# Nyström attention and a gated MLP in one program: two batches per inverse iteration, an inverse root moved to GpSimd

## The chip, the cores and the metric

The program runs on one core of a Trainium2 chip. The metric is the device time of one launch in microseconds (us). The core has five engines with a queue each: TensorE (PE in the profile; PEld is its weight load), VectorE (DVE), ScalarE (ACT), GpSimd (POOL) and SyncE (SP), which issues the DMAs here. The engines wait for one another by semaphores. SBUF is the memory on the core, PSUM the banks that TensorE writes.

## What is computed

Eight batches with eight heads go through an approximate attention, whose output is the input of a gated MLP on 4608 tokens (cut from the reference):

```
q, k, v: [8, 8, 576, 64]; m = 32 landmarks, each the mean of 18 rows
A  = softmax(q @ k_lm.T)       # 576 x 32
Bm = softmax(q_lm @ k_lm.T)    # 32 x 32
C  = softmax(q_lm @ k.T)       # 32 x 576
Z  = Bm.T / (norm1(Bm) * norminf(Bm) + 1e-6)
for _ in range(6):
    Z = 2 * Z - Z @ Bm @ Z
attn = A @ Z @ C @ v           # per batch and head; heads side by side: x, 4608 x 512
xn   = x / sqrt(mean(x * x) + 1e-6) * rms_g
out  = (silu(xn @ w_gate) * (xn @ w_val)) @ w_out    # 512 -> 1536 -> 512
```

The weights come as float64 and are decoded on the chip. Products that need it are made in three passes of a high and a low part (hi and lo).

## The kernel before, in words

The MLP runs in two parts. In the first part ("early"), nine chunks of 512 tokens go through a third of the hidden width (four slices of 128). In the second part, from about 485 us on, all tokens go twice through the other two thirds (the names px, pz, pw, swfs). The change touches nothing of the second part.

A chunk (`mlp_chunk`, L252) is a stream of matmuls: psg and psv of each slice, then pso. It needs the normalised x of its tokens as xhi and xlo. Batches have 576 tokens and chunks 512, so chunk i needs batch i (and the end of batch i-1). The attention of later batches is laid into the chunks' matmul streams.

**The order of work** is written by a planner at build time, the class `Mixer` (L212). It keeps a clock and a list of streams (Python generators). `fill` takes a chunk's matmuls one after the other, adds 0.216 to the clock for each, and gives every stream a turn. A stream issues some instructions and then yields: a pair (cost, wait) adds the cost to the clock and puts the stream off by wait times `slack`; a negative number only puts it off. `drain` jumps the clock ahead until a condition holds. `slack` is 1.8 up to chunk 0 and 1.3 from there. TensorE's instructions keep this order. The other engines' instructions are ordered by the framework's scheduler; the streams `seconds` and `newtons` have high priority (`urgent`). A tile's buffer count (`bufs`) says how many tiles of a name can be alive: the next one waits until the oldest is free.

The streams of the attention, per batch b:

- `stage1(b, g)` for the two halves g of four heads: sums over the landmarks' rows (lmT, L342), scores sC, sA and psB on TensorE, maxima (mx), exponentials on ScalarE (E, eb), Bm (L392), and a transposed copy tA (L395). At its start it issues the loads of the next half's q, k and v.
- `back()` inside it, a stream of its own for each half: softmax of A on tA (maximum L406, subtraction on GpSimd L407, exponential, sum L410, multiplication on GpSimd L414, transposition into AT L416), its split into hi and lo (AS, L418, L419), transposition of E (sE, sF, copied to ET, EL), and pCV = C v, scaled into the right-hand side of PV (L443).
- `newton(b)`: norms of Bm, then five steps that multiply Z's factors and C v together (pn on TensorE, PV on VectorE, L496 to L498), a sixth (VZ, L502), and the product pW with its split Whi, Wlo (L520, L521). Each step waits for the one before.
- `second(b)`: pO = A times that product, for g = 0 and 1, copied to xr (L554) and squared (sq, L556). Then, after a wait of `OWL` (`OWL0` for batch 0), the sums of squares (pss, L562), a transposition (sqT), pms and ms (L571), and the inverse root of ms on 128x18 elements (the loop's body is the four VectorE instructions L578 to L581):

```python
nc.vector.tensor_single_scalar(ri, ms.bitcast(I32), 1, op=ALU.logical_shift_right)
nc.vector.tensor_scalar(ri, ri, -1, 0x5F3759DF, op0=ALU.mult, op1=ALU.add)
for c in (1.0, 0.375**2):
    ...
```

  It is spread over the heads' rows (Rb, L583), transposed (Rt), and multiplied into xr with the gain (L587). xr is stored to DRAM for the second part (L591).
- `finish(b, which)` splits xr into xhi (ScalarE, L614) and xlo (VectorE and GpSimd, L616) of the chunks that it belongs to: chunk b at once, chunk b+1 when chunk b is about to start.

The gates: `firsts` (L638) starts batch b's first half when newton(b-2) is done and its second half when second(b-2) is done (batch 1 at once, batch 2 after newton(1)). `newtons` takes the batches one by one, each after both halves' scores, and waits for both halves' pCV before the steps. `seconds` starts second(b) when newton(b) is done and chunk b-1 has started. After the matmuls of chunk i the loop at L683 drains until second(i+1) is issued.

Of the kernel before, what the change touches and what calls it, by code (L numbers as in the profile page):

```python
# [9 lines left out]
F32 = mybir.dt.float32  # L10
# [8 lines left out]
P = 128  # L19
# [4 lines left out]
OWL0 = 7.0  # L24
# [11 lines left out]
OWL = 7.0  # L36
# [13 lines left out]
TAB = 2  # L50
# [25 lines left out]
TINY = 1.0513759e-09  # L76


@with_exitstack
def nystrom_moe_kernel(  # L80
# [47 lines left out]
    VZ = cst.tile([P, G, 3 * D], F32, name="VZ")  # L128
# [169 lines left out]
    with tc.tile_pool(name="ap", bufs=1, side="right") as ap, tc.tile_pool(  # L298
# [36 lines left out]
        def stage1(b, g):  # L335
            nt = state[b]
            qk = loaded.pop((b, g))
            vt, vl_ = loaded.pop((b, g, "v"))
# [7 lines left out]
            if b > 0 and nxt[0] < B:  # L346
                load_qk(*nxt)
                load_v(*nxt)
# [25 lines left out]
            rs = sm.tile([P, 2], F32, name="rs", tag="rs")  # L374
# [5 lines left out]
            E = ap.tile([P, S], F32, name="E", tag="E", bufs=2)  # L380
# [4 lines left out]
            eb = sm.tile([P, M], F32, name="eb", tag="eb")  # L385
# [6 lines left out]
            (nc.scalar.mul if BMA else nc.vector.tensor_scalar_mul)(nt["Bm"][:, g, :], eb, rs[:, 1:2])  # L392
            tA = ap.tile([P, NB, M], F32, name="tA", tag="tA", bufs=TAB)
            for e in range(2):
                nc.vector.transpose(  # L395
                    tA[:, e * (NB // 2) : (e + 1) * (NB // 2), :].rearrange("p n m -> p (n m)"),
                    sA[e],
                )
            yield 1.3, 0.0
            if g == 1:  # L400
                stage["front"] = b

            def back():
                yield -BW * mix.slack
                mA = sm.tile([P, NB], F32, name="mA", tag="mA")
                nc.vector.tensor_reduce(mA, tA, axis=AX.X, op=ALU.max)  # L406
                nc.gpsimd.tensor_sub(tA, tA, mA.unsqueeze(2).broadcast_to([P, NB, M]))  # L407
                nc.scalar.activation(tA, tA, AF.Exp, scale=SC)
                sumA = sm.tile([P, NB], F32, name="sumA", tag="sumA")
                nc.vector.tensor_reduce(sumA, tA, axis=AX.X, op=ALU.add)  # L410
                nc.vector.tensor_scalar_add(sumA, sumA, 1e-9)
                rA = sm.tile([P, NB], F32, name="rA", tag="rA")
                nc.vector.reciprocal(rA, sumA)
                nc.gpsimd.tensor_mul(tA, tA, rA.unsqueeze(2).broadcast_to([P, NB, M]))  # L414
                AT = ap.tile([P, S], F32, name="AT", tag="AT", bufs=ATB)
                nc.vector.transpose(AT, tA.rearrange("p n m -> p (n m)"))  # L416
                AS = ap.tile([P, 2, S], F32R, name="AS", tag="AS", bufs=ASB)
                nc.scalar.copy(AS[:, 0], AT)  # L418
                nc.vector.tensor_sub(AS[:, 1], AT, AS[:, 0].bitcast(F32))  # L419
                nt["AT"][g] = AS  # L420

                sE = pa.tile([P, 4, P], F32, name="sE", tag="pa")
                for ch in range(4):
                    tp(sE[:, ch], E[:, ch * P : (ch + 1) * P], ident)
                sF = pa.tile([2 * M, P], F32, name="sF", tag="pa")
                tp(sF, E[:, 4 * P :], ident)
                ET = ap.tile([P, 4, P], F32, name="ET", tag="ET", bufs=ETB)
                EL = ap.tile([2 * M, P], F32, name="EL", tag="EL", bufs=ETB)
                nc.scalar.copy(ET, sE)
                nc.scalar.copy(EL, sF)  # L430
                yield 0.65, SW2
                pCV = pa.tile([P, D], F32, name="pCV", tag="pa")
                for ch in range(5):
                    for h in range(4):
                        r = slice(h * M, (h + 1) * M)
                        mm(
                            pCV[r, :],
                            ET[:, ch, r] if ch < 4 else EL[:, r],
# [4 lines left out]
                (nc.scalar.mul if CVA else nc.vector.tensor_scalar_mul)(nt["PV"][:, g, M:], pCV, rs[:, 0:1])  # L443
                yield 0.85, 0.2
                done[b] = done.get(b, 0) + 1
                if done[b] == 2:
                    stage["first"] = b
# [11 lines left out]
        def newton(b):  # L459
            nt = state[b]  # L460
            Bm = nt["Bm"]
            BT = sm.tile([P, 2, M], F32, name="BT", tag="BT", bufs=1)
# [3 lines left out]
            sums = sm.tile([P, 4], F32, name="nsum", tag="nsum")  # L466
            nc.vector.tensor_reduce(
                sums[:, 0:2], Bm, axis=AX.X, op=ALU.add, apply_absolute_value=True
            )
            nc.vector.tensor_reduce(  # L470
                sums[:, 2:4], BT, axis=AX.X, op=ALU.add, apply_absolute_value=True
            )
            sb = sm.tile([P, 4, M], F32, name="nsb", tag="nsb", bufs=1)
            nc.vector.tensor_copy(sb, sums.unsqueeze(2).broadcast_to([P, 4, M]))
            sbt = sm.tile([P, 4, M], F32, name="nsbt", tag="nsbt", bufs=1)
# [578 lines left out]
```

## Time and profile before

| | us |
|---|---|
| median of 3 runs | 1066.85 |
| lowest and highest | 1066.61, 1067.96 |
| profiled execution | 1064.71 |
| its span in the trace | 1062.8 |
| TensorE busy | 992.8 |
| VectorE busy | 743.4 |
| ScalarE busy | 486.7 |
| GpSimd busy | 89.5 |

The profile is of one execution. Its span runs from the first to the last instruction; the execution's own time is 1.9 us longer. The views that are quoted below: a string of 40 digits (busy tenths in 40 slices of 26.6 us); busy time of each engine in chosen stages, with the number of instructions behind it, the clock that TensorE was granted (1.00 is full), the share of the DMA engines and GB/s; waits (engine, line and tile that waited, what released it, total us, times, longest); groups of instructions (line, engine, operation, out<-in, shape, xcount, then busy us and mean ns of one, then idle time before them); and the timeline (start, duration, engine, line, operation, tiles, in brackets the idle time just before it and what ended it).

### The profile page before, as it was taken

The page shows a single profiled execution, that of the slowest core. Times are in us where ns is not written, and L with a number is a line of the kernel's source. Part 1 is how long each engine was busy: PE and PEld are TensorE (multiplying, and loading weights), DVE is VectorE, ACT ScalarE, POOL GpSimd, SP SyncE. Part 2 cuts the span into 40 slices and gives each one's busy share as a digit, 9 for nine tenths or more (in the row PEclk, how much of TensorE's full clock was granted, in tenths as well). Part 3 has the DMA queues.
Part 4 walks back from the last instruction along what each step waited for, and adds up shares of the span by engine and source line. Part 5 has one row for each costly group of instructions (what it writes and reads, how often), then busy time and mean ns, then how long its engine had stood idle before and what let it go on. Part 6 is the DMA issues. An engine that isn't in the chain of part 4 may idle for free.

```text
span 1062.8 us, 17582 instructions
## 1 busy us (share of the span) xinstructions
PE 992.8 (93%) x6918; PEld 833.9 (78%) x6918; DVE 743.4 (70%) x1503; ACT 486.7 (46%) x990; POOL 89.5 (8%) x86
## 2 busy tenths in 40 slices
PE   5639689989989999999999999999999999999998
PEld 3326466556767777787989899998999989899997
DVE  7799586797494551988995675747897475675743
ACT  3534556555454543455645352433744334352431
POOL 2243121211020210100000000000000000000000
PEclk7659889999999999999999999999999999999999
DMA  9244343434140211543533505134250432505122
GB/s 335 100 150 136 133 164 105 153 104 163 43 142 11 86 45 40 187 145 119 189 123 135 178 1 179 51 129 155 64 178 21 159 96 83 179 1 178 50 70 80
DMA packets 62946, 123.82 MB, mean 117 GB/s; under 512 B 5520, under 2 KB 27024, under 8 KB 61840
## 3 DMA queue, kind: packets, MB, share of 16 engines
q1 hardware_dynamic: 62864, 122.71, 34.0%
q8 instruction: 54, 0.88, 0.3%
q14 instruction: 28, 0.23, 0.1%
HBM read 84.94 MB, written 37.75 MB: 115 GB/s over the span
## 4 chain that ended last, share of the span: by engine, by line
PE 72%; DVE 15%; DMA 6%; issue 2%; ACT 2%; POOL 2%; SPq 0%; ACTq 0%; POOLq 0%; DVEq 0%
PE pso L141 23%; PE px L141 18%; PE pz L141 9%; PE psg L141 6%; PE psv L141 5%; PE pw L141 5%; DMA qk<-in_q_dram 2%; PE pO L141 2%; DMA srawv<-in_moe_w_val_dram 1%; DVE lmT L342 1%; PE pn L141 1%; DVE xr L587 1%; DVE h L275 1%; PE sC L141 1%; PE pss L141 1%
## 5 line engine op out<-in xcount | busy, mean ns | idle before, releaser
L141 PE MATMUL pso<-whio,h 128*128 128x512 f32 x288 | 96.2, 402 | 5.8 <-DVE h L275 4.7
L141 PE MATMUL pso<-solo,h 128*128 128x512 f32 x432 | 100.4, 390 | 0.0
L829 ACT CAST x<-xf 128x768 fp32r<-128x768 f32 x84 | 68.1, 833 | 69.7 <-DVE xf L847 54.2
L141 PEld LDWEIGHTS pso<-solo,h 128*128 128x128 f32 x432 | 81.0, 188 | 16.3
L141 PE MATMUL pso<-sowhio,h 128*128 128x512 f32 x288 | 90.9, 390 | 0.0
L141 PE MATMUL psg<-xhi,whig 128*128 128x512 f32 x144 | 60.7, 421 | 25.6 <-ACT xhi L614 25.6
L945 DVE TENSOR_TENSOR ob<-ob,pso 128x512 f32<-128x512 f32 x72 | 48.8, 684 | 49.1 <-PE pso L141 48.1
L830 DVE TENSOR_TENSOR x<-xf,x 128x768 fp32r<-128x768 f32 x84 | 79.2, 953 | 5.0 <-ACT x L829 5.0
L877 DVE TENSOR_TENSOR h<-c,h 128x384 fp32r<-128x384 f32 x96 | 53.2, 555 | 37.3 <-ACT h L876 37.2
L898 ACT COPY c<-px 128x384 f32<-128x384 f32 x48 | 23.1, 481 | 108.6 <-PE px L141 108.6
L141 PEld LDWEIGHTS pso<-whio,h 128*128 128x128 f32 x288 | 53.4, 188 | 20.4 <-DVE h L275 6.0
L876 ACT CAST h<-c 128x384 fp32r<-128x384 f32 x96 | 49.4, 515 | 34.5 <-DVE c L887 28.3
L141 PE MATMUL psg<-xlo,whig 128*128 128x512 f32 x144 | 60.6, 421 | 4.7 <-DVE xlo L616 4.0
L141 PEld LDWEIGHTS pso<-sowhio,h 128*128 128x128 f32 x288 | 54.1, 188 | 11.0
L141 PE MATMUL psg<-xhi,wlog 128*128 128x512 f32 x144 | 60.5, 420 | 0.0
L141 PE MATMUL psv<-xhi,wlov 128*128 128x512 f32 x144 | 58.1, 403 | 0.0
L141 PE MATMUL px<-x,swfs0c 128*128 128x384 f32 x288 | 58.0, 335 | 0.0
L141 PE MATMUL psv<-xlo,whiv 128*128 128x512 f32 x144 | 58.0, 403 | 0.0
L141 PE MATMUL px<-x,swfs1c 128*128 128x384 f32 x288 | 57.8, 334 | 0.1
L141 PE MATMUL px<-x,swfs2c 128*128 128x384 f32 x288 | 57.8, 335 | 0.0
L141 PE MATMUL psv<-xhi,whiv 128*128 128x512 f32 x144 | 57.8, 401 | 0.0
L141 PE MATMUL pso<-wloo,h 128*128 128x512 f32 x144 | 57.4, 398 | 0.0
(224 smaller groups left out, 2231.6 us busy)
## 6 DMA issues: line engine op xcount, KB each, us to landing
xd<-xr SPq DMA_DIRECT2D x8, 1152.0 KB, 4.3
pd<-ob SPq DMA_DIRECT2D x36, 256.0 KB, 2.1
xf<-xd SPq DMA_DIRECT2D x8, 1152.0 KB, 7.5
ob<-pd SPq DMA_DIRECT2D x36, 256.0 KB, 3.5
pe<-ob SPq DMA_DIRECT2D x36, 256.0 KB, 2.6
ob<-pe SPq DMA_DIRECT2D x36, 256.0 KB, 2.8
out_dram<-ob SPq DMA_DIRECT2D x36, 256.0 KB, 2.7
vt<-in_v_dram SPq DMA_DIRECT2D x16, 512.0 KB, 4.0
```

Of the source, the lines that this page charges most:

```text
L141: tc.keep_in_program_order(nc.tensor.matmul(*args, **kw))
L275: nc.vector.tensor_sub(h2, s, h1.bitcast(F32))
L342: nc.vector.tensor_reduce(lmT[:, z], qk[z].rearrange("p h (m c) -> p h m c", c=LM), axis=AX.X, op=ALU.add)
L587: last = nc.vector.scalar_tensor_tensor(xr[:, kk], xr[:, kk], gsb[:, kk : kk + 1], Rt, op0=ALU.mult, op1=ALU.mult)
L829: nc.scalar.copy(t[:, 0], src)
L830: nc.vector.tensor_sub(t[:, 1], src, t[:, 0].bitcast(F32))
L876: nc.scalar.copy(hi, s)
L877: nc.vector.tensor_sub(lo, s, hi.bitcast(F32))
L898: nc.scalar.copy(c1, px)
L945: nc.vector.tensor_add(ob, ob, bank.pop(t))
```

## The change

1. `GROUPS`: batches 3 and 4, and 5 and 6, go through `newton` together. Bm, PV, VZ and all its tiles have room for two batches; `bmm` makes all their matmuls into one bank, and each VectorE instruction covers both. Batches 0, 1, 2 and 7 stay alone.
2. New gates in `firsts`: with the pairs, batch 3 and later wait for second(max(1, b-3)) instead of newton(b-2) and second(b-2); batch 4 also for newton(2).
3. `back` takes both halves of a batch at once from batch 3 (`BOTH`) on, with its waits `BW2` and `SW3`. E, tA, AT and the reciprocals rs become tiles of a whole batch; E and tA have one buffer, where each half had one of two.
4. The split of AT into AS moves out of `back` into a stream `splits` of its own, one batch at a time, after pO of the batch before; AS has one buffer of a whole batch.
5. The loads of v for batch 4 and later move from `stage1` to the end of `back` of the batch before.
6. xr has one buffer instead of two (`XRB`). The W step of `newton` waits until pO of the batch before the group is issued.
7. `OWL` and `OWL0` go from 7 to 3.
8. The inverse root: instead of two rounds of four VectorE instructions, three Newton rounds of four GpSimd instructions. Rb is then a copy on VectorE.

```diff
-OWL0 = 7.0
+OWL0 = 3.0
-OWL = 7.0
+OWL = 3.0
-TAB = 2
+TAB = 1
+XRB = 1
+GROUPS = ((0,), (1,), (2,), (3, 4), (5, 6), (7,))
+BOTH = 3
+SW3 = 2.6
+BW2 = 5.5
...
-    VZ = cst.tile([P, G, 3 * D], F32, name="VZ")
+    VZ = cst.tile([P, 2 * G, 3 * D], F32, name="VZ")
...
                 load_qk(*nxt)
-                load_v(*nxt)
+                if nxt[0] <= BOTH:
+                    load_v(*nxt)
...
+            if g == 0:
+                nt["E"] = ap.tile([P, 2, S], F32, name="E", tag="E", bufs=1)
+                nt["tA"] = ap.tile([P, 2, NB, M], F32, name="tA", tag="tA", bufs=TAB)
+                nt["rs"] = sm.tile([P, 2, 2], F32, name="rs", tag="rs")
+                nt["AT"] = ap.tile([P, 2, S], F32, name="AT", tag="AT", bufs=3)
...
-            mix.add(back())
+            if b < BOTH:
+                mix.add(back(b, nt, g, 1))
+            elif g == 1:
+                mix.add(back(b, nt, 0, 2))
+
+        def back(b, nt, g0, n):
...
+            if n == 2 and b + 1 < B:
+                for g in range(2):
+                    load_v(b + 1, g)
+            yield 0.85 * n, 0.2
...
+        def splits():
+            for b in range(B):
+                while stage["first"] < b or stage["small"] < b - 1:
+                    yield -0.3
+                nt = state[b]
+                AS = nt["AS"] = ap.tile([P, 2, 2, S], F32R, name="AS", tag="AS", bufs=1)
+                for g in range(2):
+                    nc.scalar.copy(AS[:, 0, g], nt["AT"][:, g])
+                    nc.vector.tensor_sub(AS[:, 1, g], nt["AT"][:, g], AS[:, 0, g].bitcast(F32))
+                stage["split"] = b
...
         def bmm(lt, rhs, n, nm):
-            ps = pa.tile([P, 2, n], F32, name=nm, tag="pa")
-            for g in range(2):
+            w = lt.shape[1]
+            ps = pa.tile([P, w, n], F32, name=nm, tag="pa")
+            for g in range(w):
...
-            while stage["first"] < b:
+            while stage["first"] < group[-1]:
                 yield -0.3
...
+            while stage["small"] < group[0] - 1:
+                yield -0.3
...
-            xr = ap.tile([P, NK, S], F32, name="xr", tag="xr", bufs=2)
+            xr = ap.tile([P, NK, S], F32, name="xr", tag="xr", bufs=XRB)
...
+                if g == 1:
+                    stage["small"] = b
                 yield 0.9, ((OWL if b else OWL0) if g == 1 else OW)
...
-            for c in (1.0, 0.375**2):
-                nc.vector.tensor_mul(r2, r1, r1)
-                nc.vector.scalar_tensor_tensor(r2, r2, c, ms, op0=ALU.mult, op1=ALU.mult)
-                nc.vector.scalar_tensor_tensor(r2, r2, -10.0 / 3.0, r2, op0=ALU.add, op1=ALU.mult)
-                nc.vector.scalar_tensor_tensor(r1, r2, 5.0, r1, op0=ALU.add, op1=ALU.mult)
+            for _ in range(3):
+                nc.gpsimd.tensor_mul(r2, r1, r1)
+                nc.gpsimd.tensor_mul(r2, r2, ms)
+                nc.gpsimd.tensor_scalar(r2, r2, -0.5, 1.5, op0=ALU.mult, op1=ALU.add)
+                nc.gpsimd.tensor_mul(r1, r1, r2)
...
-            (nc.scalar.mul if RBA else nc.vector.tensor_scalar_mul)(Rb, r1.unsqueeze(2).broadcast_to([P, NB, M]), 0.375**2)
+            nc.vector.tensor_copy(Rb, r1.unsqueeze(2).broadcast_to([P, NB, M]))
...
+            for i, group in enumerate(GROUPS[1:]):
+                while i > 0 and stage["newton"] < GROUPS[i - (group[0] > 2)][-1]:
+                    yield -0.3
+                new_state(group[0])
+                for b in group:
+                    while b > 2 and (stage["second"] < max(1, b - 3) or (b == 4 and stage["newton"] < 2)):
+                        yield -0.3
+                    yield from stage1(b, 0)
+                    yield from stage1(b, 1)
...
-                while stage["newton"] < b or stage["chunk"] < b - 1:
+                while min(stage["newton"], stage["split"]) < b or stage["chunk"] < b - 1:
...
         mix.add(newtons(), True)
+        mix.add(splits(), True)
```

More of the change, by code (lines that the diff above doesn't have):

```diff
@@ L384, in stage1 @@
                 )
-            eb = sm.tile([P, M], F32, name="eb", tag="eb")
+            eb = sm.tile([P, M], F32, name="eb", tag="eb", bufs=1)
             nc.scalar.activation(
@@ L431, in back @@
-                yield 0.65, SW2
-                pCV = pa.tile([P, D], F32, name="pCV", tag="pa")
+                    tp(sE[:, ch], nt["E"][:, g, ch * P : (ch + 1) * P], ident)
+                nc.scalar.copy(ET[:, g], sE)
+            sF = pa.tile([2 * M, 2, P], F32, name="sF", tag="pa")
+            for g in gs:
+                tp(sF[:, g], nt["E"][:, g, 4 * P :], ident)
+            nc.scalar.copy(EL[:, gsl], sF[:, gsl])
+            yield 0.65 * n, SW2 if n == 1 else SW3
+            pCV = pa.tile([P, 2, D], F32, name="pCV", tag="pa")
@@ L433, in back @@
+            for g in gs:
+                vt, vl_ = loaded.pop((b, g, "v"))
                 for ch in range(5):
@@ L457, in bmm, with newton @@
             return ps
[L459 to L462, printed above, removed]
+        def newton(group):
+            nt = state[group[0]]
+            n = 2 * len(group)
+            Bm = nt["Bm"][:, :n]
+            BT = sm.tile([P, 4, M], F32, name="BT", tag="BT", bufs=1)[:, :n]
             nc.vector.transpose(
@@ L521, in newton @@
             nc.vector.tensor_sub(Wlo, pW, Whi.bitcast(F32))
-            nt["W"] = Whi, Wlo
+            for b in group:
+                state[b]["W"] = Whi, Wlo
             yield 0.5, WW
         def new_state(b):
-            state[b] = {
-                "Bm": sm.tile([P, 2, M], F32, name="Bm", tag="Bm"),
-                "PV": sm.tile([P, 2, M + D], F32, name="PV", tag="PV", bufs=3),
-                "AT": [None, None],
-            }
-        def first(b):
-            new_state(b)
-            for g in range(2):
-                yield from stage1(b, g)
+            group = next(gr for gr in GROUPS if b in gr)
+            if b == group[0]:
+                tiles = {
+                    "Bm": sm.tile([P, 4, M], F32, name="Bm", tag="Bm", bufs=2),
+                    "PV": sm.tile([P, 4, M + D], F32, name="PV", tag="PV", bufs=3),
+                }
+                for i, c in enumerate(group):
+                    state[c] = dict(tiles, at=2 * i)
         state = {}
@@ L634, in nystrom_moe_kernel, with newtons @@
         nc.sync.dma_start(gsb, rms_g.rearrange("(k p) -> p k", p=P))
[L636 removed]
+        stage = {"small": -1, "split": -1, "front": -1, "first": -1, "newton": -1, "second": -1, "chunk": -1, "g": -1}
         def firsts():
[L639 to L640 removed]
+            for i, group in enumerate(GROUPS[1:]):
+                while i > 0 and stage["newton"] < GROUPS[i - (group[0] > 2)][-1]:
                     yield -0.3
[L642 to L653 removed]
+                new_state(group[0])
+                for b in group:
+                    while b > 2 and (stage["second"] < max(1, b - 3) or (b == 4 and stage["newton"] < 2)):
+                        yield -0.3
+                    yield from stage1(b, 0)
+                    yield from stage1(b, 1)
+        def newtons():
+            for group in GROUPS:
+                while stage["front"] < group[-1]:
+                    yield -0.3
+                yield from newton(group)
+                stage["newton"] = group[-1]
         def seconds():
             for b in range(B):
[L657 removed]
+                while min(stage["newton"], stage["split"]) < b or stage["chunk"] < b - 1:
                     yield -0.3
```

126 lines of the change are left out of this document (54 added, 72 removed).

## Prediction

> **What bounds the kernel now.** I read the page's slices first, then the busy time by stage, then what TensorE waited for, then the places of the long waits in order of time.
>
> ```profile
> span 1062.8 us, 17582 instructions
> PE   5639689989989999999999999999999999999998
> ```
>
> The span is 1062.8 us, and this execution took 1064.71 us. The last digits of PE are all 9: from the twelfth slice on TensorE is hardly idle. What can be won lies in the first ten slices. The stages, with cuts at the starts of the first chunks of the MLP (columns: PE, PEld, DVE, ACT, POOL busy with counts, granted clock, DMA share, GB/s):
>
> ```profile
> 0.00:67.00 67.00, 32.73 (x447) 20.34 (x447) 55.98 (x145) 26.25 (x65) 17.10 (x21) 0.64 0.58 204
> 67.00:122.00 55.00, 51.20 (x471) 35.94 (x474) 39.52 (x69) 27.14 (x56) 18.21 (x13) 0.91 0.41 130
> 122.00:134.00 12.00, 0.80 (x25) 0.51 (x9) 12.00 (x43) 4.67 (x15) 2.27 (x2) 0.62 0.43 154
> 134.00:142.00 8.00, 6.13 (x16) 4.63 (x17) 8.00 (x14) 4.43 (x11) 3.75 (x4) 0.51 0.36 148
> ...
> 201.00:269.00 68.00, 60.77 (x695) 41.19 (x694) 57.29 (x148) 39.82 (x85) 17.16 (x16) 0.95 0.44 154
> 269.00:485.00 216.00, 211.92 (x1527) 161.54 (x1526) 135.37 (x320) 102.22 (x222) 22.98 (x23) 1.00 0.26 91
> ```
>
> Before 67 there is no MLP matmul; the front is a latency chain with VectorE at 55.98 of 67 us. From 122 to 134 TensorE stands (0.80 of 12) while VectorE is full (12.00 of 12). The 8 us after it run at a clock of 0.51. Then TensorE is the bound, with 7.2 us idle in 201 to 269 and 4.1 in 269 to 485. What it waited for up to 485:
>
> ```profile
> PE psg L141 <- ACT xhi L614: 25.6, 3, 13.9
> PE pn L141 <- DVE PV L498: 8.8, 9, 1.6
> ```
>
> 25.6 us are three waits of a chunk's first matmul for its input. The timeline shows where the two long ones end and what stood before them:
>
> ```profile
> 46.63 2.01 PE L141 MATMUL pss<-sq,ones 128*32 128x288 f32 x16
> 52.80 0.40 PE L141 MATMUL pms<-sqT,sel 128*128 128x18 f32 x2 [0.56 <-ACT ET L429]
> 67.14 0.80 PE L141 MATMUL psg<-xhi,whig 128*128 128x512 f32 x1 [13.93 <-ACT xhi L614]
> ...
> 111.93 0.30 PE L141 MATMUL pO<-AS,Wlo 64*128 64x288 f32 x2
> 119.68 1.18 PE L141 MATMUL pss<-sq,ones 128*32 128x288 f32 x16
> 134.06 0.79 PE L141 MATMUL psg<-xhi,whig 128*128 128x512 f32 x1 [11.26 <-ACT xhi L614]
> 137.73 0.80 PE L141 MATMUL psg<-xlo,whig 128*128 128x512 f32 x1 [1.82 <-DVE xlo L616]
> ```
>
> So chunk 0 waits for batch 0's normalisation, and chunk 1 for batch 1's: 11.26 + 1.82 = 13.1 us. Inside that chain, on VectorE:
>
> ```profile
> 53.24 0.18 DVE L571 TENSOR_SCALAR ms<-pms 128x18 f32<-128x18 f32 x1
> 62.26 0.44 DVE L583 TENSOR_SCALAR Rb<-r 128x576 f32<-128x576 f32 x1
> 123.45 0.14 DVE L571 TENSOR_SCALAR ms<-pms 128x18 f32<-128x18 f32 x1
> 131.24 0.45 DVE L583 TENSOR_SCALAR Rb<-r 128x576 f32<-128x576 f32 x1
> 0.00:485.00 485.00, 19.64 (x88) 0.92 0.37 126
> ```
>
> From ms to Rb it takes 9.0 us in batch 0 and 7.8 in batch 1, though the last row (the same view by stage, of VectorE's instructions on tile r alone) gives eleven instructions per batch 19.64 / 8 = 2.46 us: two shifts of 0.17, as long as ms, the copy to Rb of 0.45, and eight steps of the iteration, 1.66 in all. The rest is other work queued between them on a full engine.
>
> **The change, part by part.**
>
> *Inverse root on GpSimd.* Each batch loses 1.66 us of VectorE, 13.3 us in all, and gains 12 GpSimd instructions on 128x18. No such instruction is in the trace. The nearest rows, and a pair of rows on the port:
>
> ```profile
> L1027 POOL MEMSET const-float32-0.0<- 128x1 f32 x1 | 0.1, 99 | 0.2 <-issue 0.2
> L616 POOL TENSOR_TENSOR xlo<-xr,xhi 128x64 fp32r<-128x64 f32 x4 | 2.9, 718 | 33.0 <-ACT xhi L614 33.0
> 230.56 1.16 POOL L414 TENSOR_TENSOR tA<-tA,rA 128x576 f32<-128x576 f32 x1 [7.43 <-DVE r L579]
> 230.71 1.05 DVE L581 SCALAR_TENSOR_TENSOR r<-r,r 128x18 f32<-128x18 f32 x1
> ```
>
> Ends: 0.10 us (the memset) and 0.72 us (128x64). The 576 elements of tA take 1.16 us, 2.0 ns each, so 18 elements cost little beside a start. I take 0.25 us, nearer to the memset, because the 128x64 subtraction runs while VectorE subtracts the other blocks of the same tile. Twelve are 3.0 us (1.2 to 8.6). With the two shifts left on VectorE, the two hand-overs (0.1 us each) and one tA instruction ahead in the queue, ms to Rb should take some 4.3 us, so batch 1 wins 7.8 - 4.3 = **3.5** us (5.3 down to a loss of 2.1).
>
> The port is why the far end is kept. In the last two rows a step on 18 elements lasts 1.05 us and ends at 231.76, when the GpSimd instruction beside it ends at 231.72. The other way round, GpSimd's small steps could each be held by a VectorE instruction with two inputs in SBUF. The Trainium skill, SBUF — State Buffer, section "Who interferes with whom", says that the pair of ports is an exclusive lock, held for the whole instruction by a VectorE instruction with two SBUF inputs or by a GpSimd instruction; the two rows agree. By that rule alone, with every step held, the move would win nothing: the second rival.
>
> *OWL and OWL0 from 7 to 3.* The pss matmuls are issued 3 x slack units of the mixer's clock after the second half of pO, not 7 x slack. In chunk 0 (slack 1.3) that is 3.9 units for 9.1. From 112.2 to 119.68 the 9.1 units took 7.5 us, so 3.9 are 3.2 us: 115.4. The squares must be there:
>
> ```profile
> 113.03 1.29 ACT L556 ACTIVATE sq<-xr 128x576 f32<-128x576 f32 x2
> ```
>
> They end at 114.3, so the new wait costs nothing as long as ScalarE is on time; I take 116.0, **3.7** earlier (0 to 5). In batch 0 (slack 1.8) the units are 5.4 for 12.6, and pms at 52.80, which now stands behind the second half of batch 1's scores and sE, should go ahead of them, soon after pss ends at 48.6: about 3.5 us earlier. With the root's 9.0 - 4.3 = 4.7 chunk 0 could start 8 us sooner. But VectorE is then the limit:
>
> ```profile
> 49.00:103.00 54.00, 34.96 (x349) 23.63 (x333) 51.15 (x113) 22.65 (x49) 21.55 (x15) 0.78 0.45 150
> ```
>
> It is idle for 2.85 of these 54 us, in which the weights are decoded and batch 1's iteration runs. What can be carried to the end of that iteration is 2.85 + 1.66 = **4.5** us (0 to 8).
>
> *Batches 3+4 and 5+6 together.* The matmuls are the same; four iterations become two, with instructions of double size, so eight chains for which TensorE can wait become six. All waits behind L498 are 8.8 us, and half of them would be the most that can go. VectorE saves the starts of 2 x 18 instructions, some 0.1 us each (ms, of 18 elements, lasts 0.14 to 0.18), 3.6 us, off the path. The merged back from batch 3 on has the same elements in fewer instructions, each twice as long; MLP matmuls hide that, and without them each batch would see at least one more GpSimd pass over tA for each of its two, 2.3 us.
>
> *One more batch in flight.* Batch 4's scores now wait for second(1) and newton(2), 6's for second(3). Batch 3's first half now also waits for second(1), which takes it out of the gap at 122 to 134. The pair's iteration must end before second(3), which chunk 3 needs:
>
> ```profile
> 231.94 0.45 DVE L583 TENSOR_SCALAR Rb<-r 128x576 f32<-128x576 f32 x1
> 268.76 0.47 PE L141 MATMUL psg<-xhi,whig 128*128 128x512 f32 x1
> ```
>
> Rb of batch 3 stood 36.8 us ahead of chunk 3's first matmul; from Rb to that matmul batch 1 took 134.06 - 131.24 = 2.8 us, so a pair that ends up to 34 us later costs nothing here.
>
> *xr with one buffer.* second(b) now waits until xr of b-1 has been split and stored. For batches 4 and 6, whose iteration is long done, it starts with the chunk, just where that store is in the air:
>
> ```profile
> xd<-xr SPq DMA_DIRECT2D x8, 1152.0 KB, 4.3
> 201.88 0.38 SPq L591 DMA_DIRECT2D xd<-xr  x1
> 204.24 1.42 ACT L554 COPY xr<-pO 128x288 f32<-128x288 f32 x4 [0.96 <-PE pO L141]
> ```
>
> At chunk 2 the store was issued at 201.88, the median landing takes 4.3 us, and second(3)'s copy ran at 204.24; with one buffer it would have waited to some 206.2. Behind it on ScalarE stand the squares and the chunk's first Silu, and TensorE stops at the second half of pO, for want of banks. I take 1.5 us at each of two chunks, **+3** (0 to 9).
>
> *At nothing:* the split of AT into AS is the same 16 copies and subtractions, later, behind the last pO of the batch before, and before a second that starts a chunk later; v of batches 4 to 7 is loaded behind pCV, on SP's queue past the qk loads and the stores of ob, the best part of a batch before use. If that cover fails, one landing is seen, like the 4.3 us above.
>
> *Later stalls.* One 3.16 us wait at 239.88 stands behind a block of urgent scaling on VectorE between two steps of newton(4):
>
> ```profile
> 239.88 0.43 PE L141 MATMUL sA<-qk,lmT 64*32 64x288 f32 x1 [3.16 <-DVE PV L443]
> 240.00:245.00 5.00, 5.00 (x61) 3.14 (x58) 3.38 (x11) 2.01 (x4) 0.92 (x1) 0.66 0.84 298
> ```
>
> Fewer chains and a lighter VectorE should take **2** us off such waits (6 off, or 10 more).
>
> **Sum:** -4.5 (front) - 3.7 (pss) - 3.5 (root) + 3 (xr) - 2 (later) = -10.7. 1064.71 - 10.7 = 1054.0 for the profiled execution; the median of the runs shown is 2.1 above it, so **1056**.
>
> **Clock.** Chunk 1's wait would shrink from 13.1 to 13.1 - 7.2 = 5.9 us. After the 3.16 us wait the clock fell (0.66 in 240 to 245), so it still falls after 5.9, and the sum has nothing for it. The Trainium skill, TensorE: Matmul & The Clock Gate, section "What's actually happening", puts the fall behind an idle window of about 3.4 us; the 0.51 after 13.1 us agrees. If the gap shrank below 3 us, the eight slow microseconds would give back up to 8 x (1 - 0.51) = 3.9.
>
> **Rivals.**
> 1. *The gap closes.* 0.10 us per GpSimd step (-1.8 more), all 8 us at the front, the clock stays up (-3.9), no wait for xr (-3), and the later waits go by 6: 10.7 + 1.8 + 3.5 + 3.9 + 3 + 4 = 26.9, about 1040. For it: nothing but latency holds chunk 1. Against: VectorE has no room before 103. Chance 0.15, as 1035 to 1047.
> 2. *The root gains nothing.* Each step is held on the port (0.7 us), the front gives only what earlier pms gives VectorE to do (1.5), and xr and later waits take 3: 3.7 + 1.5 - 3 = 2.2, within 2 us of before. Chance 0.10.
> 3. *Slower: VectorE fills up under the extra batch.* The place is chunks 1 and 2:
>
> ```profile
> 133.00:240.00 107.00, 96.69 (x1192) 64.70 (x1199) 89.33 (x221) 60.84 (x129) 22.59 (x21) 0.94 0.39 134
> 0.00:485.00 485.00, 43.02 (x32) 0.92 0.37 126
> 0.00:485.00 485.00, 50.54 (x80) 0.92 0.37 126
> 0.00:485.00 485.00, 19.92 (x80) 0.92 0.37 126
> ```
>
> VectorE has 107 - 89.3 = 17.7 us free there. The other rows are its work on lmT, tA and mx in all eight batches: (43.0 + 50.5 + 19.9) / 8 = 14.2 us of each batch's scores and back. That much of batch 4 is pulled ahead, and its share of the iteration with it. It decides when this passes 17.7 us: then the pair's steps wait behind it as at 239.88, 3.2 us and a cold 1.5 each. Four such waits, 19 us, against the 13.7 won before them and with xr's 3: about 8 slower, 1075. For it: the margin is thin, and VectorE was full from 122 to 134. Against: 1.66 us per batch is taken off, and MLP matmuls stand between the steps. Chance 0.20.
>
> **How the numbers follow.** Forecast 0.55 (1048 to 1063). A measurement of this kernel can tell about 0.2%, 2.1 us, from no change. Faster: 0.55 + 0.15 = 0.70; same 0.10; slower 0.20. The range 1043 to 1071 leaves out the lower half of rival 1 and about half of rival 3. The forecast's own is 1048 to 1063.
>
> **What would show it.** pss of batch 1 within 4.5 us behind pO; ms to Rb under 5 us in batches 0 and 1, GpSimd steps near 0.25; chunk 0's first psg at 59 to 64; chunk 1's wait for xhi under 8 us; xr's first copy waiting for a store or a split in batches 4 and 6. I am wrong if chunk 0 starts no earlier, if the GpSimd steps are 0.6 us or more, or if waits for PV grow past 15 us between 140 and 270.

## The result, and the profile after

| | before | after |
|---|---|---|
| median of the runs beside one another (us) | 1067.4 | 1086.9 |
| lowest and highest after | | 1085.3, 1087.7 |
| ratio, 95% interval | | 1.0181 [1.0163, 1.0198] |
| profiled execution | 1064.71 | 1086.63 |
| span in the trace | 1062.8 | 1084.8 |
| TensorE busy | 992.8 | 996.0 |

The changed kernel is 1.8% slower; the forecast was 1.0% faster. The span grew by 22.0 us. TensorE's busy time grew by 3.2 us and its idle time by 18.8 (1084.8 - 996.0 = 88.8, before 70.0). The page's slices of the changed kernel (40 slices, 27.1 us each now) show where:

```profile
span 1084.8 us, 17500 instructions
PE   5569599597979999999999999999999999999998
```

Up to the seventh slice it looks much as before. Behind that, where the string before had nothing but 8 and 9, there are now a 5 and two 7s: slices 8, 10 and 12, from 190, 244 and 298 us on. The busy time by stage, cut at the starts of chunks 1, 2, 3 and at the end of chunk 3, says how much. First the kernel before, then the changed one (columns: length of the stage, then PE, PEld, DVE, ACT, POOL busy with counts, granted clock, DMA share, GB/s):

```profile
134.10:200.60 66.50, 62.87 (x788) 42.65 (x788) 53.15 (x133) 34.44 (x75) 11.83 (x11) 0.94 0.36 120
200.60:268.80 68.20, 60.97 (x695) 41.25 (x695) 57.55 (x148) 40.02 (x86) 17.13 (x16) 0.95 0.44 155
268.80:318.50 49.70, 47.00 (x441) 34.25 (x441) 32.73 (x85) 24.49 (x56) 7.92 (x9) 1.00 0.27 93
```

```profile
127.10:197.30 70.20, 57.66 (x655) 39.95 (x655) 50.75 (x118) 37.78 (x79) 15.34 (x21) 0.91 0.40 134
197.30:271.40 74.10, 60.55 (x743) 42.91 (x743) 46.85 (x95) 34.51 (x69) 15.20 (x20) 0.89 0.31 111
271.40:348.70 77.30, 67.43 (x796) 47.15 (x796) 51.69 (x120) 35.91 (x81) 19.26 (x24) 0.87 0.25 86
```

Length less PE's busy time gives the idle time: 3.6, 7.2 and 2.7 us in the three chunks before, 12.5, 13.6 and 9.9 after. That is 22.5 us more, against 4.0 less ahead of chunk 1 (49.3 before, 45.3 after). Chunk 1 starts 7.0 us earlier than before (127.1 for 134.1), chunk 2 still 3.3 earlier, and chunk 3 is 2.6 late. The 7 of slice 12 is a third place, inside chunk 3: from 298.3 to 325.4 TensorE is idle for 5.65 us, in smaller waits of which the longest, 3.4 us, is for ScalarE. Chunk 3 is so long (77.3 for 49.7) since matmuls that used to run ahead of it now run in it: its count of matmuls is 796 for 441. What TensorE waited for up to 520 us, after the change (engine, line, tile waited for: us in total, times, longest):

```profile
PE psg L146 <- ACT xhi L652: 35.9, 4, 11.4
PE pn L146 <- DVE PV L533: 11.0, 13, 2.1
PE psg L146 <- DVE xlo L654: 7.6, 4, 2.5
```

The waits for PV, which the forecast feared, are small. The waits of a chunk's first matmuls for their input are four now, and the timeline shows the two new ones, at chunks 2 and 3, behind the old one at chunk 1:

```profile
117.36 0.40 PE L146 MATMUL pms<-sqT,sel 128*128 128x18 f32 x2 [0.76 <-DVE sqT L601]
127.08 0.80 PE L146 MATMUL psg<-xhi,whig 128*128 128x512 f32 x1 [9.31 <-ACT xhi L652]
...
188.23 0.40 PE L146 MATMUL pso<-wloo,h 128*128 128x512 f32 x1
188.47 0.29 PE L146 MATMUL pms<-sqT,sel 128*128 128x18 f32 x2
...
197.28 0.79 PE L146 MATMUL psg<-xhi,whig 128*128 128x512 f32 x1 [8.20 <-ACT xhi L652]
200.56 0.80 PE L146 MATMUL psg<-xlo,whig 128*128 128x512 f32 x1 [2.48 <-DVE xlo L654]
...
263.85 0.39 PE L146 MATMUL pso<-whio,h 128*128 128x512 f32 x1
264.08 0.29 PE L146 MATMUL pms<-sqT,sel 128*128 128x18 f32 x2
271.35 0.80 PE L146 MATMUL psg<-xhi,whig 128*128 128x512 f32 x1 [6.98 <-ACT xhi L652]
274.58 0.80 PE L146 MATMUL psg<-xlo,whig 128*128 128x512 f32 x1 [2.44 <-DVE xlo L654]
```

In both new places pms, the last step of second() on TensorE, stands at the very end of the chunk's last matmuls (pso). The root, Rb, Rt, the scaling and the split then run with nothing on TensorE, as at chunk 1: 8.20 + 2.48 and 6.98 + 2.44 = 20.1 us, where the kernel before had 0.44 + 0.81 at chunk 2 and none at chunk 3. And each of them cools the clock: in the first 7.7 us of chunk 2 the same view gives a granted clock of 0.50, and 0.50 again in the first 7.7 us of chunk 3.

```profile
197.28:205.00 7.72, 5.24 (x44) 2.75 (x46) 6.14 (x9) 3.71 (x8) 4.01 (x4) 0.50 0.37 153
```

Why second(2) and second(3) are late: second(b) needs newton(b), whose last instruction is Wlo. On VectorE's timeline, before and after, the three rows are batches 1, 2 and 3 (after the change, 3 and 4). The pair's Wlo comes 48.5 us later than that of batch 3 did. Batch 1's comes 0.9 us earlier, and batch 2's 1.8 us later, although chunk 1 now starts 7.0 us earlier: it stands 44.7 us behind the chunk's start, where it stood 35.9 behind it.

```profile
103.55 0.42 DVE L521 TENSOR_TENSOR Wlo<-pW,Whi 128x256 fp32r<-128x256 f32 x1
169.99 0.39 DVE L521 TENSOR_TENSOR Wlo<-pW,Whi 128x256 fp32r<-128x256 f32 x1
198.08 0.39 DVE L521 TENSOR_TENSOR Wlo<-pW,Whi 128x256 fp32r<-128x256 f32 x1
```

```profile
102.63 0.42 DVE L558 TENSOR_TENSOR Wlo<-pW,Whi 128x256 fp32r<-128x256 f32 x1
171.77 0.39 DVE L558 TENSOR_TENSOR Wlo<-pW,Whi 128x256 fp32r<-128x256 f32 x1
246.57 0.69 DVE L558 TENSOR_TENSOR Wlo<-pW,Whi 128x512 fp32r<-128x512 f32 x1 [1.90 <-ACT Whi L557]
```

The pair's iteration starts when batch 4's scores are done, and these came when they always had: its two halves' scores on TensorE at 181.5 and 203.0 us, before at 179.9 and 205.6. Its steps (pn) then wait for batch 4's pCV as well:

```profile
225.72 0.65 PE L146 MATMUL pCV<-vt,ET 128*32 128x64 f32 x32
230.68 0.86 PE L146 MATMUL pn<-PV 32*32 32x96 f32 x32
```

So newton(3), which ran in chunk 1 before, left that chunk. Chunk 1's last pso started at 188.6 instead of 199.8: 7.0 us of that is the chunk's earlier start, the rest is that it had less to fill it. second(2) came only 5.0 us earlier (its pms at 188.47, before at 193.45), since newton(2) came no earlier, and so it now ended behind the chunk. newton(3, 4) ended in chunk 2, so second(3) had only the chunk's end left.

### The profile page after: what moved, and what is told of

Read it like the earlier page. It is cut to its first block, busy times and chain, and to the rows that moved or that the text cites. A ratio compares the mean times of both kernels' runs of the same rounds, so it can differ in the third digit from the quotient of the medians.

```text
span 1084.8 us, 17500 instructions
## 1 busy us (share of the span) xinstructions
PE 996.0 (92%) x6918; PEld 838.2 (77%) x6918; DVE 727.7 (67%) x1373; ACT 489.5 (45%) x982; POOL 108.7 (10%) x172
## 4 chain that ended last, share of the span: by engine, by line
PE 73%; DVE 14%; DMA 4%; ACT 3%; POOL 3%; issue 3%; SPq 0%; POOLq 0%; ACTq 0%; DVEq 0%
PE pso L146 24%; PE px L146 18%; PE pz L146 9%; PE psg L146 6%; PE psv L146 5%; PE pw L146 5%; PE pO L146 2%; DVE xr L625 2%; DMA qk<-in_q_dram 2%; DVE lmT L347 1%; PE pn L146 1%; DMA qk<-in_k_dram 1%; DVE h L280 1%; PE pCV L146 1%; PE sC L146 1%
## 5 line engine op out<-in xcount | busy, mean ns | idle before, releaser
L146 PE MATMUL psg<-xhi,whig 128*128 128x512 f32 x144 | 62.4, 434 | 36.8 <-ACT xhi L652 35.9
L146 PE MATMUL psg<-xlo,whig 128*128 128x512 f32 x144 | 62.8, 436 | 8.0 <-DVE xlo L654 7.6
L146 PEld LDWEIGHTS psg<-xhi,whig 128*128 128x128 f32 x144 | 29.3, 204 | 44.5 <-ACT xhi L652 36.5
```

Of the source, the lines that this page charges most:

```text
L146: tc.keep_in_program_order(nc.tensor.matmul(*args, **kw))
```

## The experiments

Two theories stood at the start. The first lays the loss on the pairs: their iteration starts when the later batch is ready, so second(3) is late, and the chunk before has lost what filled it. The second lays it on the small edits: shorter waits and the root's place change the order that the planner writes, and put work of later batches behind. Each kernel ran in rounds beside the kernel before on the same chip, and the ratios are to that.

**The pairs undone.** All other edits stay. The gates of batches 5 to 7 in `firsts` are worked out from `GROUPS`, though, and move with it: there batches 5 and 6 wait for newton(2) and batch 7 for newton(4), here each batch b waits for newton(b-2).

```diff
-GROUPS = ((0,), (1,), (2,), (3, 4), (5, 6), (7,))
+GROUPS = tuple((b,) for b in range(8))
```

> The changed kernel with every batch alone in the inverse iteration (eight groups of one); gates, single buffers, merged back, OWL 3 and the root on GpSimd stay. Theory 1 (pairing): newton(3) no longer waits for batch 4's scores, so its product is ready near 200 us and not at 246.6, second(3) no longer ends at chunk 2's end, and newton(3) is filler in chunk 1 again. First matmul of chunks 2 and 3 waits under 3 us each for xhi, and most of the 19.5 us goes: 1062 to 1072. Theory 2 (OWL 3 lets the planner's drain end before the gap is filled): still 1080 to 1088. Theory 3 (single buffers, new gates, the split stream): still 1080 to 1088.

Measured: 1069.16 us, 1.0012 [0.9993, 1.0032]. Some 18 us of the loss are gone, so the first theory has nearly all of it. But the kernel is only back where it was: all the other edits together win nothing. Wlo of batch 3 comes at 209.5, and chunk 3 has no wait. Chunk 2 still has one, and it starts when it did in the changed kernel (197.28):

```profile
197.08 0.80 PE L146 MATMUL psg<-xhi,whig 128*128 128x512 f32 x1 [4.38 <-ACT xhi L652]
```

With 1.84 us for xlo behind it, 6.2 of the changed kernel's 10.7 us at chunk 2 stand here too. They are not the pairs': newton(2) hasn't followed chunk 1's earlier start here either (Wlo of batch 2 at 170.5, chunk 1 at 126.7).

**One pair at a time.** Either only (3, 4) or only (5, 6) is kept:

```diff
-GROUPS = ((0,), (1,), (2,), (3, 4), (5, 6), (7,))
+GROUPS = ((0,), (1,), (2,), (3, 4), (5,), (6,), (7,))
```

> The changed kernel with only batches 3 and 4 paired; 5 and 6 alone. Theory 1a: this pair holds chunk 3's input, so nearly all of the loss is here: 1080 to 1090. Theory 1b: half of it, 1073 to 1080.

```diff
-GROUPS = ((0,), (1,), (2,), (3, 4), (5, 6), (7,))
+GROUPS = ((0,), (1,), (2,), (3,), (4,), (5, 6), (7,))
```

> The changed kernel with only batches 5 and 6 paired; 3 and 4 alone. Theory 1a: batch 5's product was ready long before its chunk, so the pair costs little: 1064 to 1074. Theory 1b: half of the loss, 1073 to 1080.

With (3, 4) alone: 1087.64, 1.0175 [1.0144, 1.0206]. With (5, 6) alone: 1069.57, 1.0015 [0.9996, 1.0035]. So the cost of pairing is that of the first pair; the second costs nothing that can be measured, and wins nothing.

**The wait without the pairing.** Batches go singly, but newton(3) waits for batch 4's scores and newton(5) for batch 6's. The instructions are those of the unpaired kernel, only later.

```diff
-                while stage["front"] < group[-1]:
+                while stage["front"] < {3: 4, 5: 6}.get(group[-1], group[-1]):
```

> e1 (every batch alone) with one wait added: newton(3) starts only when batch 4's scores are out, newton(5) only after batch 6's. Nothing is merged. Theory 1a (the pair loses by its wait): most of the loss of the changed kernel comes back, 1080 to 1090, with chunks 2 and 3 waiting for xhi as there. Theory 1b (it loses by its doubled instructions or tiles): as e1, 1066 to 1073.

Measured: 1083.67, 1.0132 [1.0101, 1.0164], against 1.0012 unpaired. So waiting alone costs some 13 us of the 18. Both waits are back, though Wlo(3) stands at 231.6 and not at 246.6:

```profile
197.34 0.79 PE L146 MATMUL psg<-xhi,whig 128*128 128x512 f32 x1 [8.18 <-ACT xhi L652]
260.45 0.80 PE L146 MATMUL psg<-xhi,whig 128*128 128x512 f32 x1 [4.96 <-ACT xhi L652]
```

The wait at chunk 2 is as long as in the changed kernel. Against the unpaired kernel it is 3.8 us longer, whatever newton(3)'s instructions are: chunk 2 starts at 197 in both, but there newton(3) and batch 4's second scores (at 191.4) still fill a part of the time ahead of it. The 5 us that are left (1.0132 to 1.0181) weren't separated. Of the 15 us between the two Wlo, 12.6 pass before the first pn (218.05 here, 230.68 in the pair): the pair waits for batch 4's pCV, and this kernel waits for batch 4's scores alone. From the first pn to Wlo the pair takes 15.9 us for 13.6, so its doubled instructions add 2.3 us to the chain.

**Batch 4's scores earlier.** The pairs stay; batch 4 no longer waits for newton(2).

```diff
-                    while b > 2 and (stage["second"] < max(1, b - 3) or (b == 4 and stage["newton"] < 2)):
+                    while b > 2 and (stage["second"] < max(1, b - 3)):
```

> The changed kernel, both pairs, but batch 4's scores no longer wait for newton(2): they follow batch 3's at once. If the pair (3,4) loses by waiting for those scores (out at 182 and 205 us in the changed kernel), they come 15 to 30 us earlier, the pair's product is ready near 215 and not at 246.6, the wait before chunk 3 goes, and 1068 to 1078 is measured. Rival (earlier scores only crowd VectorE in chunk 1 and delay newton(2), so chunk 2 waits longer): 1082 to 1095.

Measured: 1074.8, 1.0068 [1.0050, 1.0087]. The pair's Wlo moves from 246.6 to 234.0, chunk 3's wait is gone, and 12 of the 18 us with it. Chunk 2's stays:

```profile
233.97 0.69 DVE L558 TENSOR_TENSOR Wlo<-pW,Whi 128x512 fp32r<-128x512 f32 x1 [1.95 <-ACT Whi L557]
```

```profile
208.44 0.80 PE L146 MATMUL psg<-xhi,whig 128*128 128x512 f32 x1 [7.02 <-ACT xhi L652]
```

So the "one more batch in flight" wasn't in flight where it was needed: the gate newton(2), which batch 4's first half had before and which the change kept, held it until 171.8, and newton(2) came no earlier than before.

**The waits OWL and OWL0.** First back to 7 in the changed kernel, then 3 alone in the kernel before, then OWL0 alone.

```diff
-OWL0 = 7.0
+OWL0 = 3.0
...
-OWL = 7.0
+OWL = 3.0
```

> The changed kernel with OWL and OWL0 back at 7. Theory 1 (pairing): the waits at chunks 2 and 3 stay or grow, since pss and pms come later: 1084 to 1095. Theory 2 (OWL 3): 1066 to 1074, with batch 2's second scores back in the gap before chunk 1. Theory 3: as theory 1.

> The kernel before with only OWL0 and OWL at 3. Theory 1 (pairing is the loss, OWL 3 is harmless): chunk 0 starts about 3 us earlier, the wait before chunk 1 loses another 2 to 4: 1058 to 1066. Theory 2: batch 2's second scores move behind chunk 1's first matmuls, newton(2) comes later, and chunk 2 waits: 1070 to 1080.

> The kernel before with OWL0 alone at 3, OWL at 7. Chunk 0 starts about 4.8 us earlier, as in e4. If the loss of e4 comes from OWL (batch 2's second scores pushed out of the gap before chunk 1), it is not here: 1061 to 1066. Rival (an earlier chunk 0 only makes the later waits longer): 1067 to 1072.

Back to 7: 1083.22, 1.0148 [1.0122, 1.0175], if anything better than with 3, though the intervals overlap. Both at 3 in the kernel before: 1074.48, 1.0057 [1.0031, 1.0083], slower, as the second theory had it. OWL0 alone: 1070.89, 1.0029 [1.0013, 1.0045], slower by 0.3%, though chunk 0 starts 4.8 us earlier than before (62.36 for 67.14):

```profile
62.36 0.80 PE L141 MATMUL psg<-xhi,whig 128*128 128x512 f32 x1 [12.84 <-ACT xhi L614]
```

```profile
103.39 0.42 DVE L521 TENSOR_TENSOR Wlo<-pW,Whi 128x256 fp32r<-128x256 f32 x1
```

newton(1) has won 0.2 us of these 4.8. What happened is seen in the second half of batch 1's scores, by Bm of that half on VectorE, in the kernel before and with OWL0 at 3:

```profile
57.56 0.23 DVE L392 TENSOR_SCALAR Bm<-eb,rs 128x32 f32<-128x32 f32 x1
```

```profile
83.12 0.23 DVE L392 TENSOR_SCALAR Bm<-eb,rs 128x32 f32<-128x32 f32 x1
```

The long wait had given the planner time to issue those scores while chunk 0's input was awaited. With a short one its drain ends first, and the scores come 26 us later, behind chunk 0's first matmuls (24 later in the changed kernel). To test that, OWL0 stays at 3, and the drain ahead of chunk 0 is held until batch 1's scores are issued:

```diff
-        mix.drain(lambda: stage["second"] >= 0)
+        mix.drain(lambda: stage["second"] >= 0 and stage["front"] >= 1)
```

> e10 (the kernel before with OWL0 at 3), and the planner drains before chunk 0 until batch 1's scores are out. Theory: pms still goes early, batch 1's second scores come back to about 51 us, newton(1) is ready 2 to 5 us before 103.4: 1061 to 1066. Rival: chunk 0 starts later again and nothing is won: 1067 to 1071.

Measured: 1065.56, 0.9966 [0.9949, 0.9982]; Wlo of batch 1 at 96.72, 6.7 us earlier than without, and chunk 1 starts at 128.83 for 136.00. By the two ratios (1.0029 and 0.9966) the gain is 0.63%, 6.7 us. But it isn't the early start that is carried on. TensorE keeps its order, and the scores now stand ahead of chunk 0:

```profile
63.22 1.14 PE L141 MATMUL sC<-qk,lmT 64*32 64x288 f32 x2 [14.40 <-issue]
67.66 0.77 PE L141 MATMUL psg<-xhi,whig 128*128 128x512 f32 x1
```

The wait for xhi has become a wait of 14.4 us in front of the scores, and chunk 0 starts no earlier than before (67.66 for 67.14). The profile names no releaser for that wait; on VectorE's timeline the landmark sums lmT of that half come at 61.78, behind the root, the scaling and the split. The scores come later than before (Bm at 73.69 for 57.56), so the theory's 51 us for them was wrong too. What is won is in newton(1): its Wlo stands 29.1 us behind chunk 0's start, 41.0 with OWL0 alone and 36.4 before. Why it is shorter than before, with later scores, isn't shown.

**The root on GpSimd, alone in the kernel before.**

```diff
-            for c in (1.0, 0.375**2):
-                nc.vector.tensor_mul(r2, r1, r1)
...
+            for _ in range(3):
+                nc.gpsimd.tensor_mul(r2, r1, r1)
+                nc.gpsimd.tensor_mul(r2, r2, ms)
+                nc.gpsimd.tensor_scalar(r2, r2, -0.5, 1.5, op0=ALU.mult, op1=ALU.add)
+                nc.gpsimd.tensor_mul(r1, r1, r2)
```

> The kernel before with only the inverse root on GpSimd (and Rb as a copy). By the steps seen in the changed kernel (0.21 to 0.24 us each, 0.3 us apart) ms to Rb takes 4 to 5 us and not 9.0 and 7.8 in batches 0 and 1: chunk 0 starts 2 to 4 us earlier, the wait before chunk 1 shrinks by 2 to 4: 1059 to 1065. Rival: VectorE fills the time with other work and nothing is won: 1066 to 1069.

Measured: 1075.72, 1.0070 [1.0045, 1.0096], slower, which neither expectation had, though chunk 1 starts 7 us earlier. The loss is behind that. VectorE's timeline in batch 5, first of the kernel before, then of this one:

```profile
338.00 0.18 DVE L571 TENSOR_SCALAR ms<-pms 128x18 f32<-128x18 f32 x1 [2.15 <-PE pms L141]
341.59 0.46 DVE L583 TENSOR_SCALAR Rb<-r 128x576 f32<-128x576 f32 x1
```

```profile
340.57 0.18 DVE L571 TENSOR_SCALAR ms<-pms 128x18 f32<-128x18 f32 x1 [2.15 <-PE pms L141]
345.95 0.46 DVE L583 COPY Rb<-r 128x576 f32<-128x576 f32 x1 [2.85 <-POOL r L581]
```

ms to Rb takes 5.4 us instead of 3.6, and VectorE stands idle for 2.85 us of it. It takes its queue in order: once Rb is at the head, it waits for the twelve GpSimd steps, and everything behind Rb waits too. In batch 0 of this kernel VectorE has work for all of that time and doesn't stand at Rb, in batch 1 it stands 1.14 us, and in the others 1.5 to 3.7. TensorE was busy through these 5.4 us, so the hold by itself costs nothing here. The next long wait of TensorE begins 9 us on and is for ScalarE, which does the exponentials of the next scores first:

```profile
358.80 0.64 PE L141 MATMUL pso<-whio,h 128*128 128x512 f32 x1 [3.59 <-ACT s L270]
```

The kernel before has no such wait in chunk 4. How the hold leads there isn't shown.

The reverse, the changed kernel with the root back on VectorE:

```diff
-            for _ in range(3):
-                nc.gpsimd.tensor_mul(r2, r1, r1)
...
+            for c in (1.0, 0.375**2):
+                nc.vector.tensor_mul(r2, r1, r1)
...
```

> The changed kernel with the inverse root back on VectorE. If the move costs 7 us here too, as alone in the kernel before (e3), by VectorE standing at Rb until GpSimd's twelve steps are through (20.6 us in the changed kernel): 1076 to 1083. Rival (the root is hidden in the gaps that the pair opens, or even helps there): 1085 to 1092.

Measured: 1088.41, 1.0196 [1.0155, 1.0237]: no gain. Chunk 0 starts 1.8 us later and chunk 1 4.6 us later than with GpSimd (63.4 and 131.7), and the time is the same within the noise. If what is lost early is made up later, GpSimd's root wins in the first two batches and loses in the others; the profiled execution doesn't show that (it took 1094.94 us, 6.5 above the median, and its chunk 8 starts 7.4 us later than the changed kernel's). To test it, the root was left on GpSimd in batches 0 and 1 alone, in two kernels:

```diff
+            if b < 2:
+                for _ in range(3):
...
+            else:
+                for c in (1.0, 0.375**2):
...
```

> e10 and the inverse root on GpSimd in batches 0 and 1 alone, where VectorE is full; from batch 2 on it stays on VectorE, where the chain takes 2.3 to 5.3 us anyway. Chunk 0 starts 5 to 7 us earlier than before, chunk 1 7 to 10: 1056 to 1064 if half of that is kept. Rival (chunk 1 then waits at its end for second(2), which has not moved): 1066 to 1070.

> e1 (every batch alone) with the root on GpSimd in batches 0 and 1 alone. If GpSimd's chain costs in the later batches, where it holds VectorE at Rb for 2 to 3.7 us each, it is 3 to 8 us under e1: 1060 to 1066. Rival (hidden there): as e1, 1067 to 1071.

In the kernel before with OWL0 at 3: 1067.53, 1.0001 [0.9979, 1.0022], for 1.0029 without; the intervals overlap, so no gain is shown. In the unpaired kernel: 1062.54, 0.9958 [0.9942, 0.9975], for 1.0012 with the root on GpSimd throughout. So the GpSimd root of batches 2 to 7 costs some 6 us there.

**Put together.** Unpaired, the root on GpSimd in batches 0 and 1 alone, and two drains held: the one ahead of chunk 0 until batch 1's scores are issued, the one behind chunk 0 until batch 2's are, whose second half the changed kernel issued at 136.1 us, behind chunk 1's start (before at 120.8, ahead of it):

```diff
-        mix.drain(lambda: stage["second"] >= 0)
+        mix.drain(lambda: stage["second"] >= 0 and stage["front"] >= 1)
...
-            mix.drain(lambda: stage["second"] > i)
+            mix.drain(lambda: stage["second"] > i and stage["front"] >= (2 if i == 0 else 0))
```

> e12, and the planner drains before chunk 0 until batch 1's scores are out and before chunk 1 until batch 2's are. Theory (scores pushed out of the wait take back the gain of the front): batch 1's second scores return to about 50 us, newton(1) is ready 3 to 6 us earlier than 102.6, chunk 1 starts 2 to 5 us earlier than 127.1, the wait before chunk 2 goes: 1052 to 1060. Rival (VectorE is full there, whatever the order): 1060 to 1065.

Measured: **1046.8, 0.9792 [0.9771, 0.9813]**, faster than both kernels and than the 1052 to 1060 that were expected. The waits of TensorE up to 520 us, and two rows of the timelines:

```profile
PE sC L146 <- issue: 14.2, 1, 14.2
PE pn L146 <- DVE PV L533: 8.5, 11, 1.7
PE pn L146 <- DVE PV L525: 8.0, 2, 5.5
PE psg L146 <- ACT xhi L659: 5.8, 1, 5.8
```

```profile
98.31 0.42 DVE L558 TENSOR_TENSOR Wlo<-pW,Whi 128x256 fp32r<-128x256 f32 x1 [0.18 <-ACT Whi L557]
```

```profile
124.55 0.79 PE L146 MATMUL psg<-xhi,whig 128*128 128x512 f32 x1 [5.79 <-ACT xhi L659]
```

The waits for xhi are 5.8 us, one, where the changed kernel had 35.9 in four. But 11.4 of these were chunk 0's, and that wait is still there under another name: the 14.2 us stand in front of batch 1's second scores, and chunk 0 starts at 68.3, 6.7 us later than in the changed kernel. What is gone is in the next three chunks, where 24.5 us have become 5.8. The one wait left for xhi is chunk 1's, and chunk 1 starts 2.5 us earlier than in the changed kernel. newton(2) has followed: its Wlo comes at 158.8 for 171.8, and chunk 2 starts at 190.0 without a wait. Which of the two drains does how much was not tried.

Two runs ask what this gain hangs on: the two drains in the changed kernel, pairs and root as they are; and the drains, waits and root of that version in the kernel before, without its gates, merged `back` and `splits`.

> The changed kernel, both pairs and the root on GpSimd throughout, with the two drains of e13. If the pair's wait is the main loss, chunks 2 and 3 still wait for xhi: 1065 to 1076, some 20 above e13. Rival (the pair lost only because everything before it was late): 1046 to 1056.

> The kernel before with OWL and OWL0 at 3, the root on GpSimd in batches 0 and 1 and the two drains. If the merged back, the gates and the split stream matter little, as e13: 1045 to 1054. If the earlier scores of the batches from 3 on are what fills the later waits: 1056 to 1066.

In the changed kernel: 1072.61, 1.0033 [1.0013, 1.0052]. The drains win 1.0181 - 1.0033 = 1.5% there, some 16 us, and the kernel is still 26 us above 1046.8; pairs and root are all that tells the two apart. In the kernel before: 1067.67, 0.9993 [0.9975, 1.0012], no gain over that kernel; neither expectation had that. So the version at 1046.8 needs something of the changed gates, the merged `back`, `splits`, the later v loads or the single buffers as well. Which of them was not tried.

## Why the prediction was wrong

**The step that failed** is "so a pair that ends up to 34 us later costs nothing here". It asked whether second(3) would still be ready, and got both sides wrong. The pair ended 48.5 us later, not 34, since batch 4's scores moved by less than 3 us and the pair's steps wait for its pCV too: the gate newton(2) in the diff held the scores, and the forecast never worked out when it opens. And the slack itself wasn't there: in the held kernel newton(3) ends only 33.6 us later than before (231.63 for 198.08), inside the 34, and that costs 13 us. The 36.8 us were read where newton(3) filled chunk 1 and newton(4) filled chunk 2. With the pair, second(2) and second(3) end behind their chunks with nothing on TensorE: 10.7 us at chunk 2, of which the pairs add 4.5, and 9.4 at chunk 3, all of it theirs, for 0 in the sum. The unpaired and the held kernel show the price: the pairs cost 18 us, and waiting alone 13 of it.

**The gains at the front, -11.7 in the sum**, would not have reached the end without the pairs either: the unpaired kernel, with all of them, is at 1.0012. 7.0 us came as far as chunk 1's start. There newton(2), which the forecast didn't look at, stayed where it was, and chunk 2 waited; and the root costs its 6 us in the later batches.

**The 4.5 us that "can be carried to the end of that iteration"** failed too: 0.9 us. Chunk 0 did start at 61.6 (59 to 64 expected), but an earlier end of the drain put batch 1's second scores behind chunk 0's matmuls. VectorE's free time, by which the step was bounded, wasn't the limit; the planner's order was. With the drain held, newton(1) ended 6.7 us earlier, but then chunk 0 didn't start early.

**pss 3.7 us earlier by OWL**: 2.5. From the last pO of batch 1 (110.14 for 111.93) to pss (115.39 for 119.68) it takes 5.25 us for 7.75, and pss as a whole comes 4.3 earlier, where 4.5 + 3.7 was the sum.

**The root**: the sizes were right and a cost was left out. The groups of GpSimd's instructions by form (count, then busy us and mean ns of one):

```profile
L617 POOL TENSOR_TENSOR r<-r,ms 128x18 f32<-128x18 f32 x24 | 5.9, 244 | 1.9
L618 POOL TENSOR_SCALAR r<-r 128x18 f32<-128x18 f32 x24 | 5.1, 213 | 2.1
```

0.21 to 0.24 us a step for the 0.25 taken. ms to Rb in batch 1 went from 7.8 to 5.1 us, a gain of 2.7 for 3.5:

```profile
118.03 0.17 DVE L609 TENSOR_SCALAR ms<-pms 128x18 f32<-128x18 f32 x1
123.12 0.46 DVE L621 COPY Rb<-r 128x576 f32<-128x576 f32 x1 [1.78 <-POOL r L619]
```

The sum priced batch 1 alone; for the others it had only "Each batch loses 1.66 us of VectorE". What it lacked is a cost in the other batches, 6 us in the unpaired kernel, which goes with the hold at Rb; of VectorE's waits in the changed kernel:

```profile
DVE Rb L621 <- POOL r L619: 20.6, 8, 3.7
```

Rival 2's way (each step held on the port, 0.7 us) wasn't seen: of the twelve steps of batch 0 two were, at 0.47 and 0.62 us, and the others took 0.21 to 0.23. Most of these ran while VectorE itself stood at Rb (2.43 us), so this is no test of a full VectorE.

**xr with one buffer, +3**: nothing measurable was seen of it. Batch 4's copy came 5 us after its pO, at 282.1, but TensorE had matmuls of the MLP in that time. No run gave xr its second buffer back, so this is read from the trace alone. A wait that the forecast hadn't looked at did show; its cause stays open. The single buffer of E alone doesn't make it, for the unpaired kernel has that buffer too and waits for E by 1.1 us at most:

```profile
308.20 0.43 PE L146 MATMUL sA<-qk,lmT 64*32 64x288 f32 x1 [3.37 <-ACT E L393]
```

**Later waits, -2**: the waits for PV went from 8.8 to 11.0 us.

**Clock**: as forecast, it stays cold behind a wait of this size: 0.50 in the 7.7 us behind the wait at 197. The Trainium skill, TensorE: Matmul & The Clock Gate, section "What's actually happening", puts the fall behind some 3.4 us of idling; the row agrees. What the forecast lacked is that the change would add two more such waits. The 3.2 us by which TensorE's busy time grew, with the same number of matmuls, may come from that; no run separates it.

**Rival 3** had the sign, a place near by (chunks 1 and 2) and the wrong mechanism. VectorE was to fill up under an extra batch. It is busy for 50.75 + 46.85 = 97.6 of 144.3 us there, 68%, where before it was 110.7 of 134.7, 82%. In the two bare chains, where TensorE did next to nothing, VectorE was busy for 4.4 of 8.2 us and 3.1 of 7.1, one step behind the other: latency was the price, not load.

## What to carry to other kernels

Joining two latency chains starts the first when the input of the later is ready: work out that time through its own gate before counting any saving, and look at what the chain that moves had been filling, since the place that it leaves can be bare. Where a planner writes the order, a shorter wait also takes away the time in which other work was issued; try to hold the planner until that work is out, and look whether the next chain then comes earlier. Small steps that move to another engine in the middle of a chain stop the engine that waits for them, with all that is queued behind: it can pay where that engine is full, and costs where it isn't.

## What the runs showed of the hardware

A GpSimd step on 128x18 elements takes 0.21 to 0.24 us, and in a chain the starts are 0.30 us apart, so that twelve take 3.6 us, in the timeline of batch 0:

```profile
54.77 0.23 POOL L619 TENSOR_TENSOR r<-r,r 128x18 f32<-128x18 f32 x1
55.07 0.22 POOL L616 TENSOR_TENSOR r<-r 128x18 f32<-128x18 f32 x1
```

VectorE's steps of this size take 0.14 to 0.18 us. GpSimd's pass over 576 elements takes 1.16 us, 2.0 ns each, so by an estimate from that row 18 elements are 0.04 us, and the rest of such a step is start. A bare wait also costs something behind itself: the granted clock was at 0.50 in the 7.7 us behind the 8.2 us wait at chunk 2, and in the 7.7 us behind the 7.0 us wait at chunk 3.
